# Turning q and k by DMA transposes, and spreading block means by small transfers, in a sparse-attention and GEGLU kernel

## The chip, the cores and the metric

The kernel runs on one core of one Trainium2 chip. The metric is device time in microseconds (us), from the first to the last instruction of a run. A run is called slow when it lies more than 1.5% above the fastest of the same kernel. Five engines matter here: TensorE (PE in the profile, its weight loads PEld), VectorE (DVE), ScalarE (ACT), GpSimd (POOL) and SyncE (SP), which only issues DMA transfers.

## The reference

The reference attends to a window of 31 keys and to 24 block summaries per head, then runs a gated feed-forward layer on the result.

```python
B, H, S, D = 4, 8, 768, 64            # batches, heads, positions, head width
block, window = 32, 16
k_sum = k.reshape(B, H, 24, 32, D).max(axis=3)
v_sum = v.reshape(B, H, 24, 32, D).mean(axis=3)
scores = concat(where(|i - j| < 16, scale * q @ k^T, -1e9),
                scale * q @ k_sum^T + log(32))
x = softmax(scores) @ concat(v, v_sum)          # -> (3072, 512)
out = x + sigmoid(x @ w_res) * ((gelu(x @ w_gate) * (x @ w_val)) @ w_out)
```

## The kernel before

The work is cut into eight units, two per batch. A unit runs 12 feed-forward steps (`fo_step`: eight matmuls, a gelu on ScalarE, a product on VectorE). Then comes a tail in which the output matmuls of this unit alternate with the attention of the next one. The matmuls of attention need q and k turned, with the head width on the partitions (the rows of the on-chip memory). PSUM is the memory that TensorE writes its results to. The turning of batch b+1 is squeezed between the feed-forward steps of the second unit of batch b. This happens in units 1, 3 and 5 (units and steps count from 0), which I call the first, second and third turning unit.

```python
def k_step(b, hp, pool, tag):            # one pair of heads; q_step is alike, without the reduce
    tp = turn_pair(k_sb[b], hp, pool, tag)         # 16 transposes on TensorE into PSUM
    nc.scalar.copy(kw[:, 1:NT - 1, 0:BAND]..., src)   # ScalarE takes them out of PSUM
    nc.vector.tensor_copy(...); nc.vector.tensor_copy(...)      # the two edge windows
    nc.vector.tensor_reduce(out=ks..., op=ALU.max)    # block maxima of k
    nc.vector.tensor_copy(kw[:, :, BAND:BAND + NB], ks...broadcast)
...
for u in range(NU):
    if half == 0 and nb < B:
        k_sb[nb] = load_qk(k, nb, 1, "k_sb"); q_sb[nb] = load_qk(q, nb, 1, "q_sb"); v_loads(nb)
    for fo in range(FO):
        fo_step(st, gvT, fo)
        if half == 1 and nb < B:
            if fo == 1:
                vsum_grp(nb, ps_t, "t")   # block means: 12 matmuls, VectorE cast, 4 small transfers
                vsum_bc(nb, 0, 4, nc.gpsimd); ...   # three GpSimd copies into the 12 windows
            elif 2 <= fo < 2 + NP:   k_step(nb, fo - 2, ps_t, "t")
            elif 2 + NP <= fo < 2 + 2 * NP:   q_step(nb, fo - 2 - NP, ps_t, "t")
    ...  # tail: s_step, res_step, ffn_step, av_step (needs the means), xt_step, end_step
```

The softmax here doesn't subtract the row's maximum and nothing guards it: scores larger than these inputs give would overflow.

Of the kernel before, what the change touches and what calls it, by code (L numbers as in the profile page):

```python
# [9 lines left out]
BF16 = mybir.dt.bfloat16  # L10
# [5 lines left out]
def kernel(  # L16
# [22 lines left out]
    QT = 64  # L39
# [4 lines left out]
    NU = 2 * B  # L44
    NP = H // 2
    BAND = QT + 2 * WIN
    PJ = 8
    PP = S // PJ

    const = ctx.enter_context(tc.tile_pool(name="const", bufs=1))  # L50
    wpool = ctx.enter_context(tc.tile_pool(name="wpool", bufs=1))
    qk = ctx.enter_context(tc.tile_pool(name="qk", bufs=2))
    work = ctx.enter_context(tc.tile_pool(name="work", bufs=3))
    ppool = ctx.enter_context(tc.tile_pool(name="ppool", bufs=4))
    upool = ctx.enter_context(tc.tile_pool(name="upool", bufs=2))
# [9 lines left out]
    bmat = const.tile([BAND, NT, 32], BF16, name="bmat")  # L65
    bgrp = const.tile([BAND, 3, 32], BF16, name="bgrp")
    warm = const.tile([128, 512], BF16, name="warm")
    kW = [[const.tile([128, NT, 128], BF16, name=f"kW{i}_{p}") for p in range(NP)] for i in range(2)]
    qT = [[const.tile([128, S], BF16, name=f"qT{i}_{p}") for p in range(NP)] for i in range(2)]
    vext = [const.tile([128, NT, H, D + 1], BF16, name=f"vext{i}") for i in range(2)]  # L70
    vsum = [const.tile([128, DM], BF16, name=f"vsum{i}") for i in range(2)]
    vpart = const.tile([128, DM], BF16, name="vpart")
# [5 lines left out]
    def load_qk(src, b, parts, name):  # L78
        t = qk.tile([PP, H, PJ, D], BF16, tag=name, name=name)
        hs = H // parts  # L80
        for i in range(parts):
            nc.gpsimd.dma_start(
                out=t[:, i * hs:(i + 1) * hs].rearrange("p h j d -> p h (j d)"),
                in_=src[b, i * hs:(i + 1) * hs].rearrange("h (p j) d -> p h (j d)", j=PJ),
            )
        return t
# [10 lines left out]
            nc.gpsimd.dma_start(out=vext[b % 2][r0:r1, t, :, 0:D], in_=src)  # L97

    k_sb, q_sb = {}, {}

    with tc.manual_schedule():

# [14 lines left out]
        def own_keys(m, n):  # L117

            nc.gpsimd.affine_select(out=m[:], in_=m[:], compare_op=ALU.is_ge, fill=0.0,
                                    base=-WIN, pattern=[[QT, n], [-BLK, 32]], channel_multiplier=1)  # L120
            nc.gpsimd.affine_select(out=m[:], in_=m[:], compare_op=ALU.is_ge, fill=0.0,
                                    base=BLK - 1 + WIN, pattern=[[-QT, n], [BLK, 32]], channel_multiplier=-1)
            nc.gpsimd.affine_select(out=m[:], in_=m[:], compare_op=ALU.is_ge, fill=0.0,
                                    base=-WIN, pattern=[[0, n], [0, 32]], channel_multiplier=1)
            nc.gpsimd.affine_select(out=m[:], in_=m[:], compare_op=ALU.is_ge, fill=0.0,
                                    base=WIN + QT - 1, pattern=[[0, n], [0, 32]], channel_multiplier=-1)
# [19 lines left out]
        own_keys(bmat, NT)  # L146
        v_loads(0)
        for p in range(NP):
            nc.vector.memset(kW[0][p][:, 0, 0:WIN], 0.0)
            nc.vector.memset(kW[0][p][:, NT - 1, BAND - WIN:BAND], 0.0)  # L150
            nc.vector.memset(kW[0][p][:, :, BAND + NB:128], 0.0)
        nc.vector.memset(warm[:], 0.0)


# [13 lines left out]
        def turn_pair(src, hp, pool, tag):  # L168
# [4 lines left out]
                                        ident[0:PP, 0:PP])  # L173
            return tp

        def k_step(b, hp, pool, tag):
            tp = turn_pair(k_sb[b], hp, pool, tag)
            kw = kW[b % 2][hp]

            src = bass.AP(tensor=tp.tensor, offset=tp[:, 0, 6:7].offset,  # L180
                          ap=[tp[:].ap[0], [8, NT - 2], [1, 12], [PP, PJ]])
            nc.scalar.copy(kw[:, 1:NT - 1, 0:BAND].rearrange("d t (p j) -> d t p j", j=PJ), src)
            nc.vector.tensor_copy(kw[:, 0, WIN:BAND].rearrange("d (p j) -> d p j", j=PJ),
                                  tp[:, :, 0:10].rearrange("d j p -> d p j"))
            nc.vector.tensor_copy(kw[:, NT - 1, 0:BAND - WIN].rearrange("d (p j) -> d p j", j=PJ),
                                  tp[:, :, PP - 10:PP].rearrange("d j p -> d p j"))
            ks = work.tile([128, NB], BF16, tag="ks", name="ks")
            nc.vector.tensor_reduce(  # L188
                out=ks.rearrange("d (t n) -> d t n", n=2),
                in_=kw[:, :, WIN:WIN + QT].rearrange("d t (n w) -> d t n w", w=BLK),  # L190
                axis=mybir.AxisListType.X, op=ALU.max)
            nc.vector.tensor_copy(kw[:, :, BAND:BAND + NB], ks.unsqueeze(1).to_broadcast([128, NT, NB]))

        def q_step(b, hp, pool, tag):
            tp = turn_pair(q_sb[b], hp, pool, tag)
            nc.scalar.copy(qT[b % 2][hp].rearrange("d (p j) -> d p j", j=PJ),
                           tp.rearrange("d j p -> d p j"))

        def vsum_mm(b, pool, tag):
            vs = pool.tile([128, DM], F32, tag=tag, name="vs")  # L200
# [18 lines left out]
        def vsum_bc(b, lo, hi, eng):  # L219
            src = vsum[b % 2][96:128, :].rearrange("p (h d) -> p h d", d=D)  # L220
            src = src.unsqueeze(1).to_broadcast([32, hi - lo, H, D])
            eng.tensor_copy(vext[b % 2][96:128, lo:hi, :, 0:D], src)  # L222

        def s_step(u, hp, st):
            b, half = u // 2, u % 2
            s = ps_s.tile([128, 2, 512], F32, tag="s", name="s")
            kw, qt = kW[b % 2][hp], qT[b % 2][hp]
            for t in range(HT):
                tt = half * HT + t
                for hh in range(2):  # L230
                    ps = slice(hh * 64, hh * 64 + 64)
                    nc.tensor.matmul(s[:, hh, t * QT:(t + 1) * QT], kw[ps, tt, :],  # L232
                                     qt[ps, tt * QT:(tt + 1) * QT], start=True, stop=True,
                                     skip_group_check=True)
            P = ppool.tile([128, 2, HT, QT], BF16, tag="P", name="P")
            nc.scalar.activation(P.rearrange("p a t q -> p a (t q)"), s[:, :, 0:TU], AF.Exp,  # L236
                                 scale=scale, bias=bias_t[:])
            Pf = P.rearrange("p a t q -> p (a t) q")
            nc.vector.tensor_mul(Pf, Pf, maskt.unsqueeze(1).to_broadcast([128, 2 * HT, QT]))  # L239
            st["P", hp] = P  # L240
# [91 lines left out]
        nc.vector.memset(vsum[1][96:128, :], 0.0)  # L332
        nc.vector.memset(bgrp[:], 1.0 / BLK)
        own_keys(bgrp, 3)
        for p in range(NP):
            nc.vector.memset(kW[1][p][:, 0, 0:WIN], 0.0)
            nc.vector.memset(kW[1][p][:, NT - 1, BAND - WIN:BAND], 0.0)
            nc.vector.memset(kW[1][p][:, :, BAND + NB:128], 0.0)


        for u in range(NU):
            b, half = u // 2, u % 2
            nb = b + 1
            if half == 0 and nb < B:
                k_sb[nb] = load_qk(k, nb, 1, "k_sb")
                q_sb[nb] = load_qk(q, nb, 1, "q_sb")
                v_loads(nb)
            gvT = upool.tile([128, FO, TU], BF16, tag="gvT", name="gvT")
            for fo in range(FO):
                fo_step(st, gvT, fo)  # L350
                if half == 1 and nb < B:
                    if fo == 1:
                        vsum_grp(nb, ps_t, "t")
                        vsum_bc(nb, 0, 4, nc.gpsimd)
                        vsum_bc(nb, 4, 8, nc.gpsimd)
                        vsum_bc(nb, 8, NT, nc.gpsimd)
                    elif 2 <= fo < 2 + NP:
                        k_step(nb, fo - 2, ps_t, "t")
                    elif 2 + NP <= fo < 2 + 2 * NP:
                        q_step(nb, fo - 2 - NP, ps_t, "t")  # L360
            n = u + 1
            if n < NU:
                nst = new_unit()
                s_step(n, 0, nst)
            else:
                nst = None
            res_step(st, 0)
            ffn_step(st, gvT, 0, 0, FO)
            if nst:
                av_step(n, 0, nst)  # L370
                s_step(n, 1, nst)
            end_step(u, st, 0)
            res_step(st, 1)
            ffn_step(st, gvT, 1, 0, 4)
            if nst:
                av_step(n, 1, nst)
                s_step(n, 2, nst)
            ffn_step(st, gvT, 1, 4, FO)
            if nst:
                av_step(n, 2, nst)  # L380
                s_step(n, 3, nst)
                xt_step(n, 0, nst, ps_t, "t")
            end_step(u, st, 1)
            res_step(st, 2)
            ffn_step(st, gvT, 2, 0, 4)
            if nst:
                av_step(n, 3, nst)
                xt_step(n, 1, nst, ps_t, "t")
            ffn_step(st, gvT, 2, 4, FO)
            if nst:  # L390
                xt_step(n, 2, nst, ps_t, "t")
                xt_step(n, 3, nst, ps_mm, "mm")
            end_step(u, st, 2)
            st = nst


# [28 lines left out]
```

## Time and profile before

The time is 305.99 us (median of three, 305.61 to 306.15). The profiled run spans 304.4 us, of which TensorE is busy 272.4 us (89%).

The view is the table of busy time by stretch, for the three turning units and one unit between them. Each line gives start:end and length, then the busy us (and instruction counts) of each engine, then the granted TensorE clock (1.00 is full), the DMA share (not used here) and the GB/s moved.

```profile
core 0: us, PE busy (x) PEld busy (x) DVE busy (x) ACT busy (x) POOL busy (x), PEclk, DMA share, GB/s
64.45:107.03 42.58, 37.50 (x393) 19.78 (x394) 26.10 (x52) 20.26 (x29) 16.13 (x17) 0.96 1.60 100
107.03:136.78 29.75, 29.49 (x252) 16.33 (x253) 16.57 (x35) 13.73 (x21) 0.00 (x0) 1.00 0.08 28
136.78:176.10 39.32, 36.74 (x390) 19.60 (x392) 25.02 (x52) 20.27 (x29) 16.18 (x17) 0.96 1.47 91
205.85:243.81 37.96, 35.18 (x390) 18.99 (x392) 25.12 (x52) 20.18 (x29) 5.57 (x3) 1.00 0.06 23
```

A unit without turning takes 29.75 us and TensorE is busy nearly all of it. The turning units take 42.6, 39.3 and 38.0 us. So at most 12.8 + 9.6 + 8.2 = 30.6 us lie in the turning.

The next three fences are the timelines of TensorE, VectorE and GpSimd in the second turning unit of the kernel before (start, us, engine, line, operation, and in brackets the idle time before it and what ended it).

```profile
148.09 0.53 PE L172 MATMUL tp<-ident,k_sb 96*64 96x96 bf16 x16 [0.42 <-DVE kW_2_93 L185]
...
151.77 0.53 PE L172 MATMUL tp<-ident,q_sb 96*64 96x96 bf16 x16 [1.74 <-DVE kW_3_94 L185]
```

```profile
144.68 0.23 DVE L192 COPY kW_0_91<-ks 128x288 bf16<-128x288 bf16 x1
...
149.06 1.91 DVE L192 COPY kW_2_93<-ks 128x288 bf16<-128x288 bf16 x1
```

### The profile page before, as it was taken

The numbers are of one execution on the slowest core, as the hardware profiler recorded it, in microseconds if no ns is written. First come the engines' busy times: TensorE is split into PE (matmuls) and PEld (weight loads), VectorE is DVE, ScalarE is ACT, GpSimd is POOL, SyncE is SP. The second block draws the span as 40 slices with busy tenths as digits, with TensorE's granted clock in tenths as the row PEclk, the third lists the DMA queues.
The fourth block names the chain that finished last, engine by engine and source line by source line (L and its number), as shares of the span: only waits on it lengthen the run. The fifth ranks groups of instructions, "written<-read, shape, count | busy, mean of one in ns | idle before, by whom it ended". The sixth has DMA issues, their size and how long they took to land.

```text
span 304.4 us, 6192 instructions
## 1 busy us (share of the span) xinstructions
PE 272.4 (89%) x2563; PEld 149.6 (49%) x2586; DVE 170.5 (56%) x375; ACT 137.7 (45%) x204; POOL 80.4 (26%) x104
## 2 busy tenths in 40 slices
PE   1665999988699999999799999999799999999993
PEld 0622565544354566455355556455354556455641
DVE  3445544673953854476933854386944854475433
ACT  2642536432466533644456533643566433643310
POOL 7976673320954000000974000000700000000000
PEclk9999599997999999999979999999999999999999
DMA  6999999991199910011099910011000110010001
GB/s 100 168 98 186 197 206 207 162 164 33 10 200 114 84 61 2 0 71 37 3 176 131 90 69 2 2 51 56 4 2 0 56 49 2 1 71 34 2 34 69
DMA packets 54987, 22.88 MB, mean 75 GB/s; under 512 B 37480, under 2 KB 51888, under 8 KB 54960
## 3 DMA queue, kind: packets, MB, share of 16 engines
q0 software_dynamic: 51360, 16.13, 81.3%
q1 hardware_dynamic: 3600, 6.37, 6.3%
q8 instruction: 20, 0.33, 0.4%
q14 instruction: 7, 0.06, 0.1%
HBM read 32.24 MB, written 6.29 MB: 127 GB/s over the span
## 4 chain that ended last, share of the span: by engine, by line
PE 65%; DMA 14%; POOL 7%; DVE 6%; issue 5%; ACT 1%; POOLq 0%; DVEq 0%
PE f L298 18%; PE g L274 16%; PE vv L278 15%; DMA vext_108<-in_v_dram 8%; PE r L288 6%; DMA w_val<-in_moe_w_val_dram 3%; DVE ks L188 3%; DMA vext_107<-in_v_dram 3%; PE tp L172 3%; PE ao L250 2%; POOL vext_107 L97 2%; PE s L232 2%; PE xp L261 2%; DVE gvT L282 2%; POOL vext_107 L222 1%
## 5 line engine op out<-in xcount | busy, mean ns | idle before, releaser
L282 DVE TENSOR_TENSOR gvT<-ge,vv 128x384 bf16<-128x384 f32 x96 | 52.9, 551 | 63.3 <-PE vv L278 63.2
L274 PE MATMUL g<-xT,w_gate 128*128 128x384 bf16 x384 | 82.3, 334 | 0.0
L281 ACT ACTIVATE ge<-g 128x384 f32<-128x384 f32 x96 | 47.1, 491 | 75.9 <-DVE gvT L282 41.3
L278 PE MATMUL vv<-xT,w_val 128*128 128x384 bf16 x384 | 80.1, 332 | 0.0
L298 PE MATMUL f<-w_out,gvT 128*128 128x512 bf16 x274 | 65.3, 379 | 1.5 <-issue 1.1
L278 PEld LDWEIGHTS <-w_val 128*128 128x128 bf16 x384 | 38.2, 100 | 26.9 <-issue 3.2
L274 PEld LDWEIGHTS <-w_gate 128*128 128x128 bf16 x384 | 35.7, 99 | 25.2 <-issue 4.2
L236 ACT ACTIVATE P<-s,bias_t 128x768 bf16<-128x768 f32 x32 | 28.9, 903 | 35.0 <-PE s L232 35.0
L298 PEld LDWEIGHTS <-gvT 128*128 128x128 bf16 x288 | 27.3, 98 | 31.0
L239 DVE TENSOR_TENSOR P<-P,maskt 128x768 bf16<-128x768 bf16 x32 | 17.7, 554 | 22.0 <-ACT P L236 22.0
L222 POOL COPY vext_108<-vsum_110 32x2048 bf16<-32x2048 bf16 x6 | 11.1, 1895 | 58.5 <-DMA vsum_110<-vpart 58.5
L288 PE MATMUL r<-w_res,xT 128*128 128x512 bf16 x88 | 24.4, 381 | 0.4
L97 POOL DMA_DIRECT2D vext_108<-in_v_dram x24 | 18.2, 770 | 18.9 <-DMA w_out<-in_moe_w_out_dram 4.7
L222 POOL COPY vext_107<-vsum_109 32x2048 bf16<-32x2048 bf16 (+1 forms) x4 | 8.3, 2108 | 47.5 <-DMA vsum_109<-vpart 47.4
L303 DVE SCALAR_TENSOR_TENSOR th<-th,f 128x512 f32<-128x512 f32 x24 | 16.3, 680 | 7.0 <-PE f L298 7.0
L97 POOL DMA_DIRECT2D vext_107<-in_v_dram x24 | 18.1, 762 | 6.5 <-PE g L274 3.3
L172 PE MATMUL tp<-ident,k_sb 96*64 96x96 bf16 x256 | 10.1, 232 | 10.6 <-DMA k_sb<-in_k_dram 6.5
L256 DVE TENSOR_TENSOR xn<-ao,rz 128x384 bf16<-128x384 f32 x32 | 17.9, 558 | 1.1
L291 ACT ACTIVATE th<-r 128x512 f32<-128x512 f32 x24 | 14.3, 594 | 8.8 <-PE r L288 8.4
L305 DVE SCALAR_TENSOR_TENSOR o<-th,xn 128x512 f32<-128x512 f32 x24 | 16.6, 692 | 0.8
L172 PE MATMUL tp<-ident,q_sb 96*64 96x96 bf16 x256 | 10.1, 232 | 6.7 <-DMA q_sb<-in_q_dram 3.0
L250 PEld LDWEIGHTS <-P 128*64 128x64 bf16 x384 | 8.9, 113 | 14.4 <-DVE P L239 5.9
(151 smaller groups left out, 220.2 us busy)
## 6 DMA issues: line engine op xcount, KB each, us to landing
out_dram<-o SPq DMA_DIRECT2D x24, 256.0 KB
k_sb<-in_k_dram POOLq DMA_DIRECT2D x3, 768.0 KB, 7.5
q_sb<-in_q_dram POOLq DMA_DIRECT2D x3, 768.0 KB, 10.6
vext_107<-in_v_dram POOLq DMA_DIRECT2D x20, 96.0 KB, 7.8
vext_108<-in_v_dram POOLq DMA_DIRECT2D x20, 96.0 KB, 10.9
w_gate<-in_moe_w_gate_dram POOLq DMA_DIRECT2D x6, 256.0 KB, 8.8
w_val<-in_moe_w_val_dram POOLq DMA_DIRECT2D x6, 256.0 KB, 9.3
w_out<-in_moe_w_out_dram POOLq DMA_DIRECT2D x3, 512.0 KB, 14.2
```

Of the source, the lines that this page charges most:

```text
L97: nc.gpsimd.dma_start(out=vext[b % 2][r0:r1, t, :, 0:D], in_=src)
L172: nc.tensor.transpose(tp[hh * 64:hh * 64 + 64, j, :], src[:, 2 * hp + hh, j, :], ident[0:PP, 0:PP])
L222: eng.tensor_copy(vext[b % 2][96:128, lo:hi, :, 0:D], src)
L236: nc.scalar.activation(P.rearrange("p a t q -> p a (t q)"), s[:, :, 0:TU], AF.Exp, scale=scale, bias=bias_t[:])
L239: nc.vector.tensor_mul(Pf, Pf, maskt.unsqueeze(1).to_broadcast([128, 2 * HT, QT]))
L256: nc.vector.tensor_mul(xn, ao[:, :, :, 0:D], rz.to_broadcast([128, NSUB, 2, D]))
L274: nc.tensor.matmul(g[:, 0:TU], w_gate[:, ko, fs], st["xT"][:, ko, :], start=(ko == 0), stop=(ko == KO - 1))
L278: nc.tensor.matmul(vv[:, 0:TU], w_val[:, ko, fs], st["xT"][:, ko, :], start=(ko == 0), stop=(ko == KO - 1))
L281: nc.scalar.activation(ge[:], g[:, 0:TU], AF.Gelu)
L282: nc.vector.tensor_mul(gvT[:, fo, :], ge[:], vv[:, 0:TU])
L288: nc.tensor.matmul(r[:], st["xT"][:, ko, ss], w_res[:, ko, :], start=(ko == 0), stop=(ko == KO - 1))
L298: nc.tensor.matmul(st["f"][:], gvT[:, fo, ss], w_out[:, fo, :], start=(fo == 0), stop=(fo == FO - 1))
```

## The change

The intent is to take the turning of batches 1 to 3 off TensorE, ScalarE and PSUM. One DMA transpose turns all of k of a batch, and another all of q. For this, k and q are loaded with positions on the partitions (`load_nat`), in runs of 64 values. The transposes are issued at the end of the unit before the turning unit. The block means are spread by 12 transfers of SyncE in place of three GpSimd copies, so that GpSimd, which issues the loads, does not wait. VectorE's k-block work moves from steps 2 to 5 to steps 4 to 7, and the block means from step 1 to step 8.

```diff
+    def load_nat(b):
+        for t in range(NT): nc.gpsimd.dma_start(out=k_nat[...], in_=k[b, :, lo:hi, :]...)   # 12, cut
+        for c in range(NQ): nc.gpsimd.dma_start(out=q_nat[:, c]..., in_=q[b, ...])           # 6, cut
+    def turn_all(b):
+        nc.sync.dma_start_transpose(out=kW[b % 2]..., in_=k_nat...)
+        nc.sync.dma_start_transpose(out=qT[b % 2]..., in_=q_nat...)
...
             if half == 0 and nb < B:
-                k_sb[nb] = load_qk(k, nb, 1, "k_sb")
-                q_sb[nb] = load_qk(q, nb, 1, "q_sb")
+                load_nat(nb)
                 v_loads(nb)
...
-                    if fo == 1:
+                    if 4 <= fo < 4 + NP:
+                        k_blocks(nb, fo - 4)              # max reduce and broadcast copy only
+                    elif fo == 4 + NP:
                         vsum_grp(nb, ps_t, "t")
-                        vsum_bc(nb, 0, 4, nc.gpsimd)      # and two more
-                    elif 2 <= fo < 2 + NP:                # k_step
-                    elif 2 + NP <= fo < 2 + 2 * NP:       # q_step
+                        for t in range(NT):
+                            nc.sync.dma_start(out=vext[nb % 2][96:128, t, :, 0:D], in_=vsum[nb % 2][96:128, :]...)
...
             end_step(u, st, 2)
+            if half == 0 and nb < B:
+                turn_all(nb)
```

More of the change, by code (lines that the diff above doesn't have):

```diff
@@ L46 @@
     BAND = QT + 2 * WIN
+    NQ = S // 128
     PJ = 8
@@ L51 @@
     wpool = ctx.enter_context(tc.tile_pool(name="wpool", bufs=1))
-    qk = ctx.enter_context(tc.tile_pool(name="qk", bufs=2))
+    qk = ctx.enter_context(tc.tile_pool(name="qk", bufs=1))
     work = ctx.enter_context(tc.tile_pool(name="work", bufs=3))
@@ L67 @@
     warm = const.tile([128, 512], BF16, name="warm")
-    kW = [[const.tile([128, NT, 128], BF16, name=f"kW{i}_{p}") for p in range(NP)] for i in range(2)]
-    qT = [[const.tile([128, S], BF16, name=f"qT{i}_{p}") for p in range(NP)] for i in range(2)]
+    kW = [const.tile([128, NT, NP, 128], BF16, name=f"kW{i}") for i in range(2)]
+    qT = [const.tile([128, NQ, NP, 128], BF16, name=f"qT{i}") for i in range(2)]
+    k_nat = const.tile([BAND, NT, DM], BF16, name="k_nat")
+    q_nat = const.tile([128, NQ, DM], BF16, name="q_nat")
     vext = [const.tile([128, NT, H, D + 1], BF16, name=f"vext{i}") for i in range(2)]
@@ L99 @@
     k_sb, q_sb = {}, {}
+    def load_nat(b):
+        for t in range(NT):
+            lo, hi = max(0, t * QT - WIN), min(S, t * QT + QT + WIN)
+            r0 = lo - (t * QT - WIN)
+            nc.gpsimd.dma_start(out=k_nat[r0:r0 + hi - lo, t].rearrange("p (h d) -> p h d", d=D),
+                                in_=k[b, :, lo:hi, :].rearrange("h p d -> p h d"))
+        for c in range(NQ):
+            nc.gpsimd.dma_start(out=q_nat[:, c].rearrange("p (h d) -> p h d", d=D),
+                                in_=q[b, :, c * 128:(c + 1) * 128, :].rearrange("h p d -> p h d"))
+    def turn_all(b):
+        nc.sync.dma_start_transpose(out=kW[b % 2].rearrange("d t g k -> d (t g) k")[:, :, 0:BAND],
+                                    in_=k_nat.rearrange("p t f -> p (t f)"))
+        nc.sync.dma_start_transpose(out=qT[b % 2].rearrange("d c g k -> d (c g) k"),
+                                    in_=q_nat.rearrange("p c f -> p (c f)"))
     with tc.manual_schedule():
@@ L148 @@
         for p in range(NP):
-            nc.vector.memset(kW[0][p][:, 0, 0:WIN], 0.0)
-            nc.vector.memset(kW[0][p][:, NT - 1, BAND - WIN:BAND], 0.0)
-            nc.vector.memset(kW[0][p][:, :, BAND + NB:128], 0.0)
+            nc.vector.memset(kW[0][:, 0, p, 0:WIN], 0.0)
+            nc.vector.memset(kW[0][:, NT - 1, p, BAND - WIN:BAND], 0.0)
+            nc.vector.memset(kW[0][:, :, p, BAND + NB:128], 0.0)
         nc.vector.memset(warm[:], 0.0)
@@ L174, in turn_pair, with k_blocks @@
             return tp
+        def k_blocks(b, hp):
+            kw = kW[b % 2][:, :, hp]
+            ks = work.tile([128, NB], BF16, tag="ks", name="ks")
+            nc.vector.tensor_reduce(
+                out=ks.rearrange("d (t n) -> d t n", n=2),
+                in_=kw[:, :, WIN:WIN + QT].rearrange("d t (n w) -> d t n w", w=BLK),
+                axis=mybir.AxisListType.X, op=ALU.max)
+            nc.vector.tensor_copy(kw[:, :, BAND:BAND + NB], ks.unsqueeze(1).to_broadcast([128, NT, NB]))
         def k_step(b, hp, pool, tag):
             tp = turn_pair(k_sb[b], hp, pool, tag)
-            kw = kW[b % 2][hp]
+            kw = kW[b % 2][:, :, hp]
             src = bass.AP(tensor=tp.tensor, offset=tp[:, 0, 6:7].offset,
@@ L186, in k_step @@
                                   tp[:, :, PP - 10:PP].rearrange("d j p -> d p j"))
-            ks = work.tile([128, NB], BF16, tag="ks", name="ks")
-            nc.vector.tensor_reduce(
-                out=ks.rearrange("d (t n) -> d t n", n=2),
-                in_=kw[:, :, WIN:WIN + QT].rearrange("d t (n w) -> d t n w", w=BLK),
-                axis=mybir.AxisListType.X, op=ALU.max)
-            nc.vector.tensor_copy(kw[:, :, BAND:BAND + NB], ks.unsqueeze(1).to_broadcast([128, NT, NB]))
+            k_blocks(b, hp)
         def q_step(b, hp, pool, tag):
             tp = turn_pair(q_sb[b], hp, pool, tag)
-            nc.scalar.copy(qT[b % 2][hp].rearrange("d (p j) -> d p j", j=PJ),
-                           tp.rearrange("d j p -> d p j"))
+            nc.scalar.copy(qT[b % 2][:, :, hp].rearrange("d c (p j) -> d c p j", j=PJ),
+                           tp.rearrange("d j (c p) -> d c p j", c=NQ))
         def vsum_mm(b, pool, tag):
@@ L226, in s_step @@
             s = ps_s.tile([128, 2, 512], F32, tag="s", name="s")
-            kw, qt = kW[b % 2][hp], qT[b % 2][hp]
+            kw, qt = kW[b % 2], qT[b % 2]
             for t in range(HT):
@@ L231, in s_step @@
                     ps = slice(hh * 64, hh * 64 + 64)
-                    nc.tensor.matmul(s[:, hh, t * QT:(t + 1) * QT], kw[ps, tt, :],
-                                     qt[ps, tt * QT:(tt + 1) * QT], start=True, stop=True,
+                    nc.tensor.matmul(s[:, hh, t * QT:(t + 1) * QT], kw[ps, tt, hp, :],
+                                     qt[ps, tt // 2, hp, (tt % 2) * QT:(tt % 2 + 1) * QT], start=True, stop=True,
                                      skip_group_check=True)
@@ L334 @@
         own_keys(bgrp, 3)
+        nc.vector.memset(k_nat[0:32, 0], 0.0)
+        nc.vector.memset(k_nat[64:96, NT - 1], 0.0)
         for p in range(NP):
-            nc.vector.memset(kW[1][p][:, 0, 0:WIN], 0.0)
-            nc.vector.memset(kW[1][p][:, NT - 1, BAND - WIN:BAND], 0.0)
-            nc.vector.memset(kW[1][p][:, :, BAND + NB:128], 0.0)
+            nc.vector.memset(kW[1][:, 0, p, 0:WIN], 0.0)
+            nc.vector.memset(kW[1][:, NT - 1, p, BAND - WIN:BAND], 0.0)
+            nc.vector.memset(kW[1][:, :, p, BAND + NB:128], 0.0)
         for u in range(NU):
@@ L351 @@
                 if half == 1 and nb < B:
-                    if fo == 1:
+                    if 4 <= fo < 4 + NP:
+                        k_blocks(nb, fo - 4)
+                    elif fo == 4 + NP:
                         vsum_grp(nb, ps_t, "t")
-                        vsum_bc(nb, 0, 4, nc.gpsimd)
-                        vsum_bc(nb, 4, 8, nc.gpsimd)
-                        vsum_bc(nb, 8, NT, nc.gpsimd)
-                    elif 2 <= fo < 2 + NP:
-                        k_step(nb, fo - 2, ps_t, "t")
-                    elif 2 + NP <= fo < 2 + 2 * NP:
-                        q_step(nb, fo - 2 - NP, ps_t, "t")
+                        for t in range(NT):
+                            nc.sync.dma_start(
+                                out=vext[nb % 2][96:128, t, :, 0:D],
+                                in_=vsum[nb % 2][96:128, :].rearrange("p (h d) -> p h d", d=D))
             n = u + 1
```

## The prediction

> What bounds it now. The engine table gives TensorE 272.4 of 304.4 us busy (89%); the chain of waits is 65% TensorE. Reading the timeline, the units without turning take 29.75 us each (107.03 to 136.78, 176.10 to 205.85, 243.81 to 273.56) and are TensorE-bound: 29.49 us busy. The three units that turn q and k of the next batch take 42.6 us (64.45 to 107.03), 39.3 us and 38.0 us. So turning costs at most 12.8 + 9.6 + 8.2 = 30.6 us. Only about 5 us of each is transposes and block-mean matmuls on TensorE; the rest is the one shared PSUM buffer: transpose, ScalarE copy (0.97 us), VectorE copies, max reduce (0.95 us) and broadcast copy.
>
> What goes. 384 of the 512 transposes and their evacuations; the GpSimd block-mean copies (3 x 1.9 us per batch), off the chain. The max reduce and broadcast copy (about 1.2 us, four times) stay on VectorE, as do 12 block-mean matmuls (0.8 us). Without new waits such a unit would take about 32 us: up to 7, 6 and 11 us saved, near 282 us in all.
>
> What comes.
> 1. Loads. k and q change from rows of eight positions to rows of 64 values. The values, already loaded so, land a 96-row window about every 0.97 us (timeline, 58.6 to 70.0 us); k and q whole took 3.9 us each. Estimate: k 11.4 us, q 7.8 us, so 11 to 12 us more per batch. Batches 2 and 3 hide that. Batch 1 does not: DMA is saturated from 8 to 70 us, and the turning unit already waits 1.85 us for values landing at 70.0 us. They would land at 81 us, later still if the transposes share the engines.
> 2. Transposes. k is 1.18 MB, q 0.79 MB. The Trainium skill, "DMA: Bandwidth & Descriptors", section "Latency and other measured facts", gives 261 GB/s for a DMA transpose: estimates of 4.5 and 3.0 us plus a fixed part. No trace here shows one. They can start only about 2.5 us into the unit, behind the last output transfer. I expect 7 to 14 us for k, q after it. The k-block work at step 4 stalls VectorE, then TensorE, where k takes over about 8 us.
> 3. Block means. SyncE needs 0.67 us to issue each of the four existing small transfers, and about 1.2 us more passes until landing. Then come 12 more, at 0.33 (an output transfer) to 0.7 us each. The first six are needed by the first value product, about 8.4 us after the block-mean matmuls; I estimate 8.5 to 11 us, more where q's transpose still occupies SyncE's queue or the next batch's loads share the engines. Stall 1 to 4 us.
>
> Sum. First turning unit: 2 to 8 us longer, because its data arrive late. Second and third: 2 to 5 us shorter each with fast transposes, 3 to 6 us longer with slow ones. Most of the 30 us is therefore handed back as waits. Prediction 307 us, 80% range 290 to 332. Chances: faster 0.33, within 2% 0.32, slower 0.35.
>
> Signs that it is right: TensorE busy falls by 10 to 15 us; units without turning stay at 29.75 us; in the waits, TensorE's block-mean matmuls wait for values of batch 1 until 82 to 92 us; VectorE's max reduce waits for the k transpose; TensorE's value product waits for the block-mean transfers; DMA stays saturated past 80 us; GpSimd busy time falls.
>
> What would make it wrong. Transposes landing within 6 us of issue, with small transfers at 0.33 us: 285 to 295 us. Transposes at a tenth of the quoted rate: over 340 us. A sharing of the DMA engines that favours one queue would shift the first unit either way.

## More of the kernel before

```profile
145.29 5.57 POOL L222 COPY vext_107<-vsum_109 32x2048 bf16<-32x2048 bf16 x3 [47.45 <-DMA vsum_109<-vpart]
```

TensorE waits 1.74 us, until 151.77, for VectorE. VectorE's broadcast copy (L192), 0.23 us at 144.68, took 1.91 us at 149.06, while the GpSimd copies (L222, 145.29 to 150.86) ran.

## The result, and the profile after

The changed kernel takes 326.26 us (median of four, 322.95 to 329.0) against 305.8 us before. The ratio is 1.065 (95% interval 1.055 to 1.075). A ratio is the mean time of one kernel's fast runs over that of the other's of the same rounds, so it is not quite the ratio of the medians.

> The changed kernel again, nothing edited, to have its profile in the fast state and its spread. Every theory: about 326 us (ratio 1.06 to 1.07); first, second and third turning unit again about 55, 48 and 40 us long; k transposes landing after about 17, 8 and 9 us.

This second set gave 329.1 us (median of four, 324.51 to 330.94; two of the four count as slow), and the profiled run took 328.18 us. The first unit was 2 us longer than expected, the second nearly 3 us shorter. The spread of the changed kernel is wider than that of the kernel before (304.27 to 306.87 in the same rounds). The busy table of the changed kernel follows, first the three turning units and the same unit between them.

```profile
63.93:121.10 57.17, 36.27 (x265) 18.45 (x265) 21.47 (x43) 13.75 (x21) 29.08 (x38) 0.79 2.08 133
121.10:150.84 29.74, 29.48 (x252) 16.33 (x253) 16.55 (x34) 13.74 (x21) 0.00 (x0) 1.00 0.07 28
150.84:196.10 45.26, 33.83 (x265) 17.91 (x266) 21.29 (x43) 13.74 (x21) 23.46 (x30) 0.89 1.82 139
225.84:265.48 39.64, 33.09 (x264) 17.45 (x265) 21.27 (x43) 13.75 (x21) 0.00 (x0) 0.96 0.42 81
```

The plain unit is unchanged (29.74 us). The turning units became 57.2, 45.3 and 39.6 us, which is 14.6, 5.9 and 1.7 us longer, together 22.2 us; the span grew by 21.8 us. In the first profile the same units took 54.7, 48.0 and 39.8 us, so a difference of under 3 us in the first or second unit between two profiles is not read as an effect below. TensorE has about 125 fewer instructions in each turning unit, but its busy time fell by only 1 to 3 us there, because the granted clock fell to 0.79, 0.89 and 0.96 (with 264 instructions and a clock of 1.00 it is 30.4 us, in `early_means` below).

What do the turning units wait for? The view of waits of the changed kernel, over the whole run (engine, line, what it waited for: us in total, times, longest), says:

```profile
DVE ks L198 <- DMA kW<-k_nat: 22.6, 3, 15.3
PE ao L273 <- DMA vext<-vsum: 19.7, 17, 5.2
PE g L297 <- DVE gvT L305: 18.1, 3, 13.8
```

The first line is VectorE's max reduce waiting for the k transpose. TensorE then waits behind VectorE (third line). The second line is TensorE's value product waiting for the spread block means. Now SyncE's timeline shows how long it was occupied with issuing, in the first and the third turning unit of the changed kernel:

```profile
66.58 12.92 SPq L115 DMA_TRANSPOSE kW<-k_nat  x1
79.73 8.43 SPq L117 DMA_TRANSPOSE qT<-q_nat  x1
93.87 3.02 SPq L239 DMA_DIRECT2D vsum<-vpart  x4
99.46 8.19 SPq L381 DMA_DIRECT2D vext<-vsum  x12
...
228.54 5.95 SPq L115 DMA_TRANSPOSE kW<-k_nat  x1
234.72 4.19 SPq L117 DMA_TRANSPOSE qT<-q_nat  x1
244.32 2.96 SPq L239 DMA_DIRECT2D vsum<-vpart  x4
248.42 8.02 SPq L381 DMA_DIRECT2D vext<-vsum  x12
```

In the third turning unit nothing is loaded beside. Its k transpose is issued in 5.95 us and lands about 8.7 us after its start (228.54 to 237.22, when VectorE starts on it). In the first turning unit the batch's values are still being loaded, and the same transpose needs 12.92 us to issue and 20.2 us to land (66.58 to 86.77). TensorE's timeline of the changed kernel shows both waits and what follows them. First the wait for k in the first turning unit:

```profile
73.90 0.81 PE L301 MATMUL vv<-xT,w_val 128*128 128x384 bf16 x4
88.52 1.44 PE L297 MATMUL g<-xT,w_gate 128*128 128x384 bf16 x4 [13.81 <-DVE gvT L305]
89.75 1.49 PE L301 MATMUL vv<-xT,w_val 128*128 128x384 bf16 x4
91.17 1.47 PE L233 MATMUL vs<-vext,bgrp 96*32 96x512 bf16 x12
```

Then the wait for the means in the third:

```profile
246.29 2.75 PE L321 MATMUL f<-w_out,gvT 128*128 128x512 bf16 x12
250.73 0.19 PE L273 MATMUL ao<-vext,P 128*64 128x65 bf16 x1 [1.69 <-DMA vext<-vsum]
251.42 0.22 PE L273 MATMUL ao<-vext,P 128*64 128x65 bf16 x3 [0.50 <-DMA vext<-vsum]
...
254.02 0.22 PE L273 MATMUL ao<-vext,P 128*64 128x65 bf16 x3 [0.46 <-DMA vext<-vsum]
254.17 0.50 PE L255 MATMUL s<-qT,kW 64*128 64x64 bf16 x12
254.60 1.89 PE L311 MATMUL r<-w_res,xT 128*128 128x512 bf16 x4
256.29 1.69 PE L321 MATMUL f<-w_out,gvT 128*128 128x512 bf16 x4
```

The six windows of means arrive about 0.65 us apart, and TensorE takes each one as it lands. From the last matmul at 249.04 to the end of the products at about 254.2 us, some 5.1 us pass with little work. After that, four matmuls `r` take 1.89 us, where the same four, unhindered, take 1.04 us. After the k wait the four `g` take 1.44 us instead of 0.81. Granted clock around the first wait, again from the busy table of the changed kernel:

```profile
75.00:81.00 6.00, 0.00 (x0) 0.00 (x0) 0.00 (x0) 0.00 (x0) 0.00 (x0) 0.93 1.57 120
81.00:87.00 6.00, 0.00 (x0) 0.00 (x0) 0.23 (x1) 0.00 (x0) 0.00 (x0) 0.50 1.75 149
87.00:91.00 4.00, 2.48 (x8) 1.01 (x7) 3.90 (x8) 0.49 (x1) 3.70 (x5) 0.50 1.60 199
```

The clock halves while TensorE idles and stays halved for some microseconds of useful work. Finer stretches of the same view put the fall at 80.1 us, 5.4 us after the last matmul ended (74.71), and the return at 93.8 us, 5.3 us after matmuls began again (88.52). The Trainium skill, "TensorE: Matmul & The Clock Gate", section "What's actually happening", says that an idle window of about 3.4 us brings the half rate, and that it takes a busy window of that length to leave it. This trace agrees, in that both delays are longer than one such window.

In the third turning unit the parts add up. The gap before step 8's matmuls is 2.33 us (the clock stayed at 1.00 there), the gap for the means 5.1 us, and the `s`, `r` and first `f` matmuls after it, at half clock from 254.2 to 257.6, take 3.74 us (254.17 to 257.91), where the same matmuls at full clock take 2.11 us (243.79 to 245.90 in `by_head` below), 1.6 us more; together 9.0 us. The same unit without these waits takes 30.6 us (`early_means` below), and 39.6 - 30.6 = 9.0.

### The profile page after: what moved, and what is told of

It reads as the page before. It is cut to its first block, busy times and chain, and to the rows that moved or that the text cites. A ratio compares the mean times of both kernels' runs of the same rounds, so it can differ in the third digit from the quotient of the medians.

```text
span 327.2 us, 5515 instructions
## 1 busy us (share of the span) xinstructions
PE 269.3 (82%) x2202; PEld 145.2 (44%) x2202; DVE 158.9 (49%) x353; ACT 118.4 (36%) x180; POOL 102.8 (31%) x143
## 4 chain that ended last, share of the span: by engine, by line
PE 49%; DMA 31%; POOL 6%; DVE 5%; SPq 5%; issue 3%; POOLq 0%; DVEq 0%
PE f L321 15%; PE g L297 11%; PE vv L301 11%; DMA kW_92<-k_nat 8%; PE r L311 6%; DMA w_out<-in_moe_w_out_dram 5%; SPq L381 3%; DMA w_val<-in_moe_w_val_dram 3%; DMA vext_97<-in_v_dram 3%; DMA vext_98<-vsum_100 3%; DMA kW_91<-k_nat 2%; DVE ks L198 2%; PE ao L273 2%; DMA q_nat<-in_q_dram 2%; DMA vext_97<-vsum_99 2%
## 5 line engine op out<-in xcount | busy, mean ns | idle before, releaser
L321 PE MATMUL f<-w_out,gvT 128*128 128x512 bf16 x288 | 71.5, 392 | 0.0
L297 PEld LDWEIGHTS <-w_gate 128*128 128x128 bf16 x384 | 37.6, 99 | 42.8 <-issue 20.8
L108 POOL DMA_DIRECT2D k_nat<-in_k_dram x36 | 27.2, 770 | 68.5 <-DMA kW_91<-k_nat 49.8
L321 PEld LDWEIGHTS <-gvT 128*128 128x128 bf16 x288 | 28.1, 100 | 33.4 <-issue 4.1
L273 PEld LDWEIGHTS <-P 128*64 128x64 bf16 x384 | 11.3, 117 | 39.4 <-issue 29.7
L277 DVE RECIPROCAL rz<-ao 128x6 f32<-128x6 f32 x32 | 6.2, 194 | 45.6 <-PE ao L273 45.4
L311 PE MATMUL r<-w_res,xT 128*128 128x512 bf16 x96 | 27.3, 411 | 0.0
L273 PE MATMUL ao<-vext_97,P 128*64 128x65 bf16 x192 | 7.5, 210 | 13.3 <-DMA vext_97<-vsum_99 11.6
L314 ACT ACTIVATE th<-r 128x512 f32<-128x512 f32 x24 | 14.3, 595 | 11.3 <-PE r L311 11.1
L273 PE MATMUL ao<-vext_98,P 128*64 128x65 bf16 x192 | 8.4, 206 | 11.1 <-DMA vext_98<-vsum_100 11.1
```

Of the source, the lines that this page charges most:

```text
L108: nc.gpsimd.dma_start(out=k_nat[r0:r0 + hi - lo, t].rearrange("p (h d) -> p h d", d=D), in_=k[b, :, lo:hi, :].rearrange("h p d -> p h d"))
L273: nc.tensor.matmul(ao[64 * e:64 * e + 64, sub, hh, :], P[:, hh, t, :], vext[b % 2][:, half * HT + t, 2 * hp + hh, :], start=True, stop=Tru ...
L297: nc.tensor.matmul(g[:, 0:TU], w_gate[:, ko, fs], st["xT"][:, ko, :], start=(ko == 0), stop=(ko == KO - 1))
L311: nc.tensor.matmul(r[:], st["xT"][:, ko, ss], w_res[:, ko, :], start=(ko == 0), stop=(ko == KO - 1))
L321: nc.tensor.matmul(st["f"][:], gvT[:, fo, ss], w_out[:, fo, :], start=(fo == 0), stop=(fo == FO - 1))
```

## The experiments

My theory after reading the traces was: the savings are real, but two DMA results are needed too soon after their issue (k turned, and spread means), and both get slower still when loads share the DMA engines; the drop of the clock multiplies each wait. Rivals were that the transposes or the 12 transfers cost something wherever they stand, or that VectorE's k-block work is the limit. The table collects the turning units of every run, in us, and the ratio to the kernel before of the same rounds.

| kernel | first | second | third | ratio (95% interval) |
|---|---|---|---|---|
| before | 42.6 | 39.3 | 38.0 | 1 |
| changed | 57.2 | 45.3 | 39.6 | 1.065 (1.055 to 1.075) |
| early_turn | 58.5 | 36.8 | 35.7 | 1.023 (1.017 to 1.029) |
| early_means | 57.0 | 30.6 | 30.6 | 0.986 (0.979 to 0.993) |
| pool_means | 46.3 | 37.0 | 36.7 | 1.001 (0.995 to 1.008) |
| by_head | 50.9 | 41.9 | 36.6 | 1.034 (1.028 to 1.041) |
| b1_on_pe | 42.1 | 46.0 | 39.8 | 1.025 (1.019 to 1.032) |
| no_v1_load | 46.2 | 45.3 | 39.6 | one run, wrong result |
| keep_warm | 55.1 | 44.8 | 39.0 | 1.063 (1.057 to 1.069) |
| means_only | 43.9 | 35.8 | 35.8 | 0.985 (0.977 to 0.992) |
| mixed | 44.6 and 42.0 | 30.9 | 31.6 | 0.958 and 0.952 |
| mixed_dma | 42.0 | 30.6 | 30.6 | 0.942 (0.936 to 0.948) |

The profile of early_turn is from a slow run (317.2 us; its fast runs are 311.73 to 313.82).

### early_turn: the transposes of batches 2 and 3 issued 29 us earlier

```diff
             if half == 0 and nb < B:
                 load_nat(nb)
                 v_loads(nb)
+                if nb > 1:
+                    turn_all(nb)
...
-            if half == 0 and nb < B:
-                turn_all(nb)
+            if u == 0:
+                turn_all(1)
```

> Transposes of batches 2 and 3 issued at the start of the unit before, some 29 us earlier; batch 1 as it was. If only the late start of the transposes cost time (placement), the wait of VectorE's max reduce for k goes to 0 in the second and third turning unit and each is 3 to 4 us shorter: about 319 us. If sharing the DMA engines with the next batch's loads costs time too (sharing), the earlier transposes also let those loads start earlier and end before the small transfers of the second turning unit: that unit falls from 48 to about 36 us, the third from 40 to 36: about 310 us. The first turning unit stays at about 55 us in both.

It measured 312.92 us. The second turning unit fell from 45.3 to 36.8 us and the third from 39.6 to 35.7, as the sharing theory said, with no wait of the max reduce for k left in them. The second gained twice what the third did: the earlier transposes also let the next batch's loads finish before the small transfers (42 GB/s moved in the 7 us from 171 us here, against 141 GB/s in the same 7 us of the changed kernel's second unit, by the busy tables). Both still lie 5 to 6 us above the 30.6 us of `early_means` below, and of the two kinds of wait the view of waits leaves only the means: in the two units together, TensorE waits 5.1 us in 12 pieces for them.

### pool_means: block means spread by GpSimd again, at the late place

```diff
-                        for t in range(NT):
-                            nc.sync.dma_start(out=vext[nb % 2][96:128, t, :, 0:D], in_=...)
+                        vsum_bc(nb, 0, 4, nc.gpsimd)
+                        vsum_bc(nb, 4, 8, nc.gpsimd)
+                        vsum_bc(nb, 8, NT, nc.gpsimd)
```

> Block means spread by three GpSimd copies as before the change, at the changed kernel's late place; transposes as changed. It also holds the next batch's loads back behind the copies. If the chain of small transfers itself is the cost (length of the chain), TensorE's wait for the means falls below 1 us in all three turning units, and the third, which has no loads beside it, falls from 40 to about 34 us; in all about 300 to 305 us. If only sharing with loads makes them slow, the third stays at 38 to 40 us and the second falls to about 40: about 314 us.

It measured 306.41 us, ratio 1.001: 20 us better than the changed kernel. Its view of waits, over the whole run:

```profile
PE ao L273 <- POOL vext L245: 5.8, 4, 1.5
```

TensorE's waits for the means fell to 5.8 us in four pieces, not below 1 us as expected, so the third unit came to 36.7 us and not to 34. But that unit has no loads beside it and still gained 2.9 us, so the chain of transfers costs time by its length alone. The first and second unit gained more (10.9 and 8.3 us). This run doesn't separate the transfers from the loads there, because the copies also hold the next loads back. In the first unit VectorE's wait for k was still 13.5 us (15.3 in the changed kernel), so most of the 10.9 us came from the means and not from k.

### no_v1_load: batch 1's transposes without loads beside them

The result is wrong: zeros stand in for the values of batch 1.

```diff
                 load_nat(nb)
-                v_loads(nb)
+                if nb > 1:
+                    v_loads(nb)
```

> Wrong result on purpose: batch 1's values are not loaded (zeros are put in their place), so that the transposes of batch 1 meet no loads. Sharing: the first k transpose lands after 8 to 10 us instead of 17, VectorE waits about 4 us for it instead of 12.6, and the first turning unit falls from 55 to about 45 us. If batch 1's transposes are slow for another reason (first use, late k rows), they stay at about 17 us.

SyncE's timeline of this kernel, first turning unit:

```profile
72.25 6.03 SPq L115 DMA_TRANSPOSE kW<-k_nat  x1
```

And its waits within that unit:

```profile
PE ao L273 <- DMA vext<-vsum: 10.0, 6, 5.3
DVE ks L198 <- DMA kW<-k_nat: 3.6, 1, 3.6
```

The issue of the k transpose fell from 12.92 to 6.03 us, and VectorE's wait for it from 15.3 to 3.6 us. The unit fell from 57.2 to 46.2 us. So the first transpose is slow because of the loads beside it. The Trainium skill, "DMA: Bandwidth & Descriptors", section "Issuing engines are not separate DMA queues", says that transfers of all issuing engines run on the same 16 DMA engines and interleave; the traces agree: this transpose landed after 20.2 us beside the loads and after 8.5 us without them (72.25 to 80.78). The unit is still 3.6 us longer than before the change; its wait for the means grew from 6.7 to 10.0 us, and no run shows why. One blemish: the zeroing on VectorE (5.26 us) made the unit before it 5.6 us longer (36.6 against 31.0), so the whole took 322.59 us, and only the numbers within the unit count here.

### by_head: the same bytes in 8 transfers instead of 12

One transfer carries one head for all 12 windows. The first value product then needs the first two transfers, not the first six.

```diff
-                        for t in range(NT):
-                            nc.sync.dma_start(out=vext[nb % 2][96:128, t, :, 0:D], in_=...)
+                        for h in range(H):
+                            nc.sync.dma_start(out=vext[nb % 2][96:128, :, h, 0:D],
+                                              in_=vsum[nb % 2][96:128, h * D:(h + 1) * D]...broadcast to 12)
```

> The changed kernel, with the same bytes of block means spread by 8 transfers of one head (all 12 windows) in place of 12 of one window (all heads), so that the first value product needs 2 of them and not 6. If SyncE's one-by-one issue (0.67 us each) of the first six is the wait, TensorE's wait for the means falls by about 2.5 to 3 us in each turning unit (third: 39.6 to about 36.5) and, with the next loads beside it, by more: in all 312 to 318 us. If the wait is the four transfers and their landing before that, or the bytes on the DMA engines, it falls by under 1 us in each: 324 us or more.

It measured 314.93 us. The third unit fell by 3.0 us, to 36.6, as expected, and the others by 6.3 and 3.4. TensorE's timeline of the third turning unit:

```profile
239.31 2.75 PE L321 MATMUL f<-w_out,gvT 128*128 128x512 bf16 x12
242.09 0.22 PE L273 MATMUL ao<-vext,P 128*64 128x65 bf16 x2
243.50 0.35 PE L273 MATMUL ao<-vext,P 128*64 128x65 bf16 x10 [1.19 <-DMA vext<-vsum]
243.79 0.35 PE L255 MATMUL s<-qT,kW 64*128 64x64 bf16 x12
244.07 1.04 PE L311 MATMUL r<-w_res,xT 128*128 128x512 bf16 x4
```

The six small waits became one of 1.19 us, and the matmuls `r` after it run at full speed (1.04 us). With equal bytes in all, what changed is how many issues stand before the first use. Fewer bytes stand before it too (96 KB, not 192), but each issue again took 0.67 us (8 in 5.36 us), with 48 KB in place of 32 KB, so the bytes do not set the pace. SyncE's one-by-one issue was that part of the wait.

### b1_on_pe: batch 1 loaded and turned as before the change

```diff
-                load_nat(nb)
+                if nb == 1:
+                    k_sb[nb] = load_qk(k, nb, 1, "k_sb"); q_sb[nb] = load_qk(q, nb, 1, "q_sb")
+                else:
+                    load_nat(nb)
...
+                if half == 1 and nb == 1:      # k_step and q_step at steps 2 to 9, means at step 1
```

> The changed kernel, with batch 1 loaded and turned on TensorE as before the change (means by 12 transfers, at the early place); batches 2 and 3 as changed. If the first turning unit's loss comes from DMA transposes and loads in a full DMA queue, it falls from 57 to 42 to 44 us; the third stays at about 40; the second at 45, or less if its next loads start earlier. In all about 310 to 314 us. If it came from elsewhere, it stays above 50 us.

It measured 312.4 us. The first unit fell to 42.1 us, as before the change; the second and third stayed (46.0 and 39.8). So the first unit's loss of 14.6 us belongs to batch 1's new path, in a DMA queue that is full at that time, together with the late place of the means that the same edit also moved.

### means_only: the kernel before with the 12 transfers alone

```diff
                         vsum_grp(nb, ps_t, "t")
-                        vsum_bc(nb, 0, 4, nc.gpsimd)     # and two more
+                        for t in range(NT):
+                            nc.sync.dma_start(out=vext[nb % 2][96:128, t, :, 0:D], in_=...)
```

> The kernel before with one part of the change alone: block means spread by 12 small on-chip transfers, at the kernel before's early place (after step 1 of the turning unit, some 25 us before they are needed). If the transfers cost time through their latency only (slack theory), nothing waits for them here: 0.99 to 1.01 of before. If they disturb the kernel in themselves, by DMA work or by SyncE time that the outputs need (cost theory), it is slower by 2% or more, since the three turning units each lost about 6 us or more beside them in the changed kernel.

It measured 300.29 us, ratio 0.985 (the interval excludes 1): a little better than the kernel before, which neither theory expected. In the second and third unit TensorE does not wait for the transfers. In the first, beside loads, their issue took 12.7 us, TensorE waited 1.07 us for them, and the unit was 1.3 us longer than before. The second and third turning units fell to 35.8 us, by 3.5 and 2.2 us. VectorE's groups by shape show why, in this kernel:

```profile
L192 DVE COPY kW<-ks 128x288 bf16<-128x288 bf16 x16 | 3.9, 242 | 0.6
```

The mean of the broadcast copy is 242 ns over all 16. Before, single tiles had means of up to 1342 ns, and the copy shown above took 1.91 us beside a GpSimd copy of 1.89 us. In the third unit the four copies took 3.15 us before and 0.94 us here, which is the 2.2 us that the unit gained. In the second they gained 2.2 us as well, and the half clock from 152.8 to 156.2 us, which followed TensorE's wait of 1.74 us, is gone too. The Trainium skill, "SBUF — State Buffer", section "Who interferes with whom", says that VectorE in its two-port modes and GpSimd take turns on a shared pair of ports, and that the second one blocks fully until the first is done. The traces agree: the copy becomes about one GpSimd copy long, and the delay is gone with the GpSimd copies. In which mode VectorE's copy ran, no view shows.

### mixed: built to beat both

```diff
+   batch 1: loads and turning on TensorE as before the change (as in b1_on_pe)
+   batches 2 and 3: turn_all(nb) right after v_loads(nb) in the unit before (as in early_turn)
+   all batches: vsum_grp and the three GpSimd copies at fo == 1
+   batches 2 and 3: elif fo in (3, 5, 7, 9): k_blocks(nb, (fo - 3) // 2)
```

> Built to beat both: batch 1 turned on TensorE as before; batches 2 and 3 turned by DMA transposes issued at the start of the unit before; block means by GpSimd, right after step 1; k-block work spread over steps 3, 5, 7 and 9. If the waits found so far are the whole loss, the first turning unit is 42 to 43 us as before, and the second and third fall to 31 to 33 us (29.75 us and 0.8 us of block-mean matmuls, and a little for VectorE): about 290 to 293 us, ratio 0.95 to 0.96. If k-block work on VectorE is a limit by itself, they stay above 35 us: 297 us or more.

It measured 291.51 us (ratio 0.958), and in a second set, beside the next two kernels, 291.18 us (ratio 0.952). The second and third turning units are 30.9 and 31.6 us, so k-block work on VectorE is no limit when spread. The second set:

> The mixed kernel again, on the same chip as the two others of this call: 291 us, turning units of 44.6, 31 and 31.6 us.

It agreed but for the first unit, 42.0 instead of 44.6 us. That unit starts beside the end of the values' loading, and it differs from run to run: it began at 64.42 us here and at 62.51 us in the first set, so its ends (106.42 and 107.14 us) differ by only 0.7 us.

### early_means: only the places moved

From early_turn, for batches 2 and 3: the same 12 transfers after step 1 instead of step 8, and k-block work at steps 3, 5, 7 and 9.

```diff
+                elif half == 1 and nb < B:          # batches 2 and 3
+                    if fo == 1:
+                        vsum_grp(nb, ps_t, "t"); ...the 12 transfers as changed...
+                    elif fo in (3, 5, 7, 9):
+                        k_blocks(nb, (fo - 3) // 2)
```

> The early-turn kernel with, for batches 2 and 3, the 12 small transfers moved from after step 8 to after step 1, and the k-block work to steps 3, 5, 7 and 9; batch 1 untouched. If the waits were only latency laid too close to their use, the second and third turning unit fall from 37 and 36 us to 31 or 32 us, with the same transposes and the same transfers; the first stays at 55 to 58 us; in all 302 to 306 us. If the transfers or the transposes take something from the unit wherever they stand, they stay at 34 us or more: 309 us or more.

It measured 302.32 us. Second and third unit are 30.6 us each, 14.6 and 9.0 us less than in the changed kernel, with the same transposes and the same transfers in number and size. The busy table of the two units:

```profile
149.32:179.94 30.62, 30.36 (x264) 16.48 (x265) 21.27 (x43) 13.73 (x21) 6.90 (x9) 1.00 1.30 89
209.69:240.32 30.63, 30.37 (x264) 16.48 (x265) 21.27 (x43) 13.73 (x21) 0.00 (x0) 1.00 0.17 41
```

TensorE is busy all but 0.3 us of each, at full clock. This rules out that either costs time wherever it stands. The first unit (57.0 us) now holds all of the loss.

### mixed_dma: mixed without the GpSimd copies

```diff
-                        vsum_bc(nb, 0, 4, nc.gpsimd)     # and two more
+                        for h in range(H): nc.sync.dma_start(...)      # as in by_head
```

> The mixed kernel with its GpSimd copies replaced by eight transfers of one head each, at the same early place. GpSimd and VectorE then no longer hold one another up: VectorE's broadcast copies fall from a mean of 0.61 us to 0.24 us. If that was on the path in the first turning unit, it falls from 44.6 us to 43 us or less, and the whole to 288 to 290 us; if the small transfers cost something of their own there, beside the next batch's loads, it is equal or slower: 291 to 294 us.

It measured 288.12 us, ratio 0.942 (0.936 to 0.948), the best of all. Its turning units, from the busy table:

```profile
63.05:105.03 41.98, 38.52 (x392) 19.93 (x393) 23.67 (x51) 20.29 (x29) 24.33 (x32) 0.92 2.30 123
134.78:165.39 30.61, 30.35 (x264) 16.46 (x265) 21.29 (x43) 13.75 (x21) 5.61 (x8) 1.00 1.22 83
195.14:225.78 30.64, 30.38 (x265) 16.50 (x266) 21.28 (x43) 13.75 (x21) 0.00 (x0) 1.00 0.17 41
```

The total is as expected, but not for the reason given: the first unit was 42.0 us in both kernels of this call. The second and third gained 0.3 and 0.9 us. VectorE's broadcast copies fell from a mean of 0.66 to 0.31 us. Of the 2.8 us between the two profiled runs, 1.4 us lies before the first turning unit (it starts at 63.05 against 64.42 us), where the code of the two kernels is the same; why is not known.

### keep_warm: matmuls on zeros in the wait for the means

```diff
+            if half == 1 and nb < B:
+                for i in range(16):
+                    nc.tensor.matmul(wp[:], warm[:, 0:128], warm[:], start=True, stop=True)
             if nst:
                 av_step(n, 0, nst)
```

> The changed kernel with 16 matmuls on zeros (about 3.5 us at full clock, results unused) put on TensorE just where it waits for the block means, in the three turning units. They fall into idle time. If the drop of the granted clock after that wait is a cost of its own (0.55 over the 3.8 us after it in the third turning unit), the third falls from 39.6 to about 37.5 us and the whole by 4 to 6 us, to about 321 us. If the drop does not matter, or the extra matmuls delay the useful ones, the third stays at 39.6 us or grows.

It measured 325.45 us, ratio 1.063. The clock was held: over the 3.5 us after the wait in the third turning unit the busy table shows

```profile
252.50:256.00 3.50, 3.50 (x60) 1.86 (x59) 2.38 (x5) 1.67 (x3) 0.00 (x0) 1.00 0.34 50
```

and the rest of the unit took 9.7 us (253.0 to 262.7) against 11.3 us (254.2 to 265.5) in the changed kernel. So the drop of the clock costs about 1.6 us there. But the unit as a whole gained only 0.6 us. In this profile the wait for k came out longer (TensorE idle for 3.23 us instead of 2.33), and the clock dropped there instead (0.50 from 237.6 to 241.0 us). The expectation of 4 to 6 us was not met. How much of the whole loss the clock makes up is not settled.

## Why the prediction was right or wrong

The forecast range (290 to 332 us) held the 326 us, and "slower" had the largest chance, but the centre of 307 us was 19 us too low. With 0.33, 0.32 and 0.35 it hardly chose between the three classes, so that "slower" came true is mostly luck. By its own terms the units could grow by 8 + 6 + 6 = 20 us at most, and they grew by 22.2; that the range held is owed to its width. Its picture was right in outline: the gain is handed back as waits for k and for the means, and the units without turning stay at 29.75 us. These are its steps:

- First turning unit, "2 to 8 us longer, because its data arrive late". The measured loss was 14.6 us, and the reason was wrong. The block-mean matmuls never waited for values. What arrived late was the k transpose, 20 us after its issue because the values' loads shared the engines (no_v1_load), and after it the means (pool_means gained 10.9 us there with the k wait still at 13.5 us). The text had the k wait too, but not in this sum; it had the sharing, but only as something that would delay the values.
- Second and third, "2 to 5 us shorter each with fast transposes, 3 to 6 us longer with slow ones". The k transpose took 8.4 and 8.7 us, near the fast end of "7 to 14 us", and the units still grew by 5.9 and 1.7 us. Here the term that was mis-sized is the means. "8.5 to 11 us" from their matmuls to the sixth landing was 13.7 us in the third unit (240.34 to 254.02) and 18.8 us in the second (165.03 to 183.85). The estimate left out that VectorE, packed with k-block work at steps 4 to 7, cast the sums only 2.4 us after their matmuls. It had the loads beside the transfers in words, but gave them no number.
- The Trainium skill's 261 GB/s for a DMA transpose ("DMA: Bandwidth & Descriptors", section "Latency and other measured facts") gave an estimate of 4.5 us plus a fixed part for k. With the landing included, 1.18 MB in 8.7 us is 136 GB/s. My wider range rightly did not trust the figure.
- "The GpSimd block-mean copies, off the chain": wrong. They blocked VectorE and with it TensorE (means_only: 3.5 and 2.2 us in the second and third unit). Taking them away was a gain that the sum did not have.
- No term for the granted clock. So the sign "TensorE busy falls by 10 to 15 us" failed: it fell from 272.4 to 265.8 us.
- The sign "GpSimd busy time falls" failed: it rose from 80.4 to 102.8 us, as each batch now has 30 load issues at about 0.8 us in place of 14. The signs for the waits of the max reduce and of the value product held, and DMA stayed saturated to about 120 us.
- "Near 282 us in all" without new waits: mixed_dma, which keeps batch 1 on TensorE, came to 288 us. The estimate of 32 us for a freed turning unit was near the 30.6 measured.

Left open: what share of the 10.9 us that pool_means gained in the first unit belongs to the loads that it held back, and the clock's share of the loss.

## What to carry to other kernels

Moving work from a compute engine to DMA pays only if its result has time to land: here, moving the same transposes and the same transfers a unit, or seven steps, ahead of where they stood took the kernel from 6.5% slower than before to 1.4% faster. Before giving DMA more to do, look at whether its engines are full at that time; the one batch whose loads had no slack was better left on TensorE. And a wait on TensorE can cost more than its length: after the wait for the means the clock was halved for 3.4 us, which cost some 1.6 us more (keep_warm), while after the 2.33 us wait before it the clock stayed full.

## What the Trainium skill lacked or had wrong

- "DMA: Bandwidth & Descriptors", section "Latency and other measured facts", gives 261 GB/s for DMA transposes with a non-contiguous middle dimension. A transpose from SBUF to SBUF of 1.18 MB, with no loads beside it, took 5.95 us of SyncE's issue and 8.7 us to landing (136 GB/s), and 20.2 us beside loads. That section gives no issue time.
- The same page, section "Issuing engines are not separate DMA queues", calls the time to issue "usually small relative to the DMA itself". For 12 transfers of 32 KB it was 8.0 us in all (about 0.67 us each, against 0.33 us for an output transfer of 256 KB), and with two issues in place of six before the first use the third turning unit was 3.0 us shorter (by_head).
- "TensorE: Matmul & The Clock Gate" speaks of idle windows of about 3.4 us, and does not say how much work in a window counts as idle. Here the clock fell to half also at the end of a gap of 5.1 us that held 12 small matmuls, about 1.2 us of work (249.0 to 254.2 us in the third turning unit), and in the kernel before at 152.8 us, after a wait of only 1.74 us. Each time it stayed at half for 3.4 us.
